# W_down and most of W_O as 512-column products in four column tiles, with six W_O rows loaded early

## The chip, the cores and the metric

The kernel runs on one core of a Trainium2 chip. The metric is the time of one execution on the device, in microseconds (us), median over runs. "Span" is the time from the first to the last instruction in the profiled execution.

## What is computed

A decoder layer with attention and a gated feed-forward network side by side, for four sequences (B = 4) with one new token each, all weights and caches in bf16:

```python
x  = A_x                                  # 4 x 1 x 512
xn = _layernorm(x)
# attention: 32 query heads, 8 key/value heads of 128, the last 4096 positions of the cache
q  = (xn @ wq) ; scores = q k^T * Dh**-0.5 ; p = softmax(scores) ; o = p v
A  = o.reshape(B, 1, 4096) @ wo           # wo: 4096 x 512
# feed-forward: 512 -> 1792 -> 512
Bf = (silu(xn @ w_gate) * (xn @ w_up)) @ w_down
return x + A + Bf                         # 4 x 1 x 512
```

The caches are 16384 positions long; only the last 4096 are read, 4 MB of K and 4 MB of V for each of the 8 key/value heads. With the weights that is 81 MB.

## The kernel before, in words

Each engine has its own program, written out in order by hand; semaphores join them. There is no scheduler: what stands first in an engine's program is done first.

**SyncE (L228 to L261)** issues nearly all loads on one queue, and the transfers run in that order: W_Q, W_gate, W_up, the two halves of the first K (L247, L248), the V of the last head group into a buffer of its own (`VL`, L250; it held W_Q before), and then for each head group g = 1 to 7 the two halves of K(g) and V(g-1) (L251 to L254), each as soon as TensorE has read what the buffer held before. There is one K buffer (two halves) and one V buffer, `VB`. Behind the last of these come W_down (L255) and W_O in five pieces, cut at the rows in `WOS` (L256, L257). W_O is laid out as 32 rows (`NR`) of 128 x 512: row e holds one of 32 slices of the contraction.

**TensorE** runs a loop of eight passes (L472), one for each head group: transposes of K (L401) and scores (L414) in turn, products that keep TensorE busy while it would wait (`spin`, L454: they multiply ones, and no result is used), then `pv` (L437) with the probabilities of the *pass before* and its V, the sums of the probabilities (L441), the shift by the maximum (L426), and `fin` (L449, L450). In `pv` the product for position t is 32 rows of output by 128 columns, in column tile t % 4 of the array, at partitions 32 (t % 4) of PSUM.

Behind the loop stands the tail: `pv` for the last group with `VL` (L491), `down` (L465), `fin`, four products that bring the attention output into the order of W_O's rows (L496), and W_O (L499 to L502). `down` and W_O go through `acc` (L459): for each row four products, one for each quarter of the 512 output columns, 4 rows of output by 128 columns. Quarter n is summed at partitions 32n to 32n + 3 of one PSUM region of 128 columns. x itself is added there too, by four fp32 products with an identity (L468); `xf` is its fp32 copy, made by VectorE (L308).

**VectorE** and **ScalarE** copy transposed K from PSUM (L322, L272), and do maxima, exponentials (L277) and normalisation (`norm`, L337 to L347). At the end VectorE writes `OP`, W_O's left operands (L363), and casts the sum to the output `y` (L365); two output transfers each on SyncE's and ScalarE's queue follow.

**GpSimd (L178 to L226)** clears buffers and makes constants; TensorE's first products wait for them (`s_const`, L217), and its first `pv` for `s_zero` (L226).

## Time and profile before

| | us |
|---|---|
| runs: median (lowest, highest) | 200.7 (200.62, 202.83) |
| profiled execution | 200.38 |
| its span, first to last instruction | 198.3 |
| TensorE busy in the span | 158.2 (80%) |
| VectorE busy | 103.4 (52%) |
| ScalarE busy | 63.0 (32%) |
| GpSimd busy | 16.7 (8%) |
| HBM read | 81.01 MB, 408 GB/s over the span |

The profile is of one execution, and 2.1 us of its time lie outside the span. In the profile's rows a line number is that of the kernel before; PE is TensorE's matmul, PEld its weight loads, DVE VectorE, ACT ScalarE, POOL GpSimd, SP SyncE. "Issue" is time in which an engine waited for nothing that the profile shows. The granted clock is the share of TensorE's full clock that the chip allowed in a stretch; q8 in the list of transfers is the queue that brings program to the engines.

### The profile page before, as it was taken

To read this page: it belongs to the slowest core of one execution; us is meant where nothing else is said; L and a number is where in the kernel's file an instruction comes from. 1 tells how busy PE (TensorE), PEld (TensorE's weight loads), DVE (VectorE), ACT (ScalarE), POOL (GpSimd) and SP (SyncE) were. 2 spreads that over 40 slices of the span, in tenths; PEclk is the share of its full clock that TensorE was granted. 3 is DMA by queue.
4 is the path that set the end of the run, shared out by engine and by line. 5 is a ranking of instruction groups with operands and counts; after the bars stand their busy time and mean duration, and the time that the engine had idled before them with its cause. 6 is when DMAs were issued, how large, how long until landed. Compare 5 with 4: busy or idle time off the path is not lost.

```text
span 198.3 us, 8645 instructions
## 1 busy us (share of the span) xinstructions
PE 158.2 (80%) x3852; PEld 136.0 (69%) x3852; DVE 103.4 (52%) x210; ACT 63.0 (32%) x85; POOL 16.7 (8%) x43
## 2 busy tenths in 40 slices
PE   0138679797998899599979986999989689978644
PEld 0138679754995697579857956698689368956544
DVE  4304047740785578147835880478468706872020
ACT  2200004503560573046415620464345115624000
POOL 8699000000000000000000000000000000000000
PEclk9999999969999999799999995799999969999975
DMA  6999999999999999999999999999999999999960
GB/s 219 430 425 437 425 426 469 433 390 433 433 418 406 430 439 439 423 449 439 420 413 446 453 420 413 436 436 420 430 466 436 397 426 473 430 394 438 409 245 1
DMA packets 4801, 81.14 MB, mean 409 GB/s; under 512 B 564, under 2 KB 568, under 8 KB 1080
## 3 DMA queue, kind: packets, MB, share of 16 engines
q1 hardware_dynamic: 4768, 81.01, 95.7%
q8 instruction: 7, 0.11, 0.2%
q14 instruction: 2, 0.02, 0.0%
q10 hardware_dynamic: 24, 0.01, 0.0%
HBM read 81.01 MB, written 0.00 MB: 408 GB/s over the span
## 4 chain that ended last, share of the span: by engine, by line
DMA 61%; PE 30%; issue 4%; DVE 2%; SPq 1%; DVEq 0%
DMA vbuf<-in_A_v_cache_dram 49%; DMA kbuf<-in_A_k_cache_dram 13%; PE ps_o L437 11%; PE ps_kt L401 8%; PE ps_s L414 3%; PE ps_s L461 3%; PE ps_kt L454 2%; PE ps_s L426 1%; PE ps_kt L441 1%; DVE kT L322 1%; PE ps_o L450 0%; PE ps_o L449 0%; DVE den L341 0%; DVE oT L346 0%; DVE oP L363 0%
## 5 line engine op out<-in xcount | busy, mean ns | idle before, releaser
L401 PE MATMUL ps_kt<-ident,kbuf 128*128 128x128 bf16 x1024 | 76.4, 221 | 2.8 <-DMA kbuf<-in_A_k_cache_dram 2.8
L322 DVE COPY kT<-ps_kt 128x1024 bf16<-128x1024 bf16 x88 | 57.6, 687 | 18.5 <-PE ps_kt L401 18.5
L401 PEld LDWEIGHTS ps_kt<-ident,kbuf 128*128 128x128 bf16 x1024 | 59.5, 98 | 5.4 <-DMA kbuf<-in_A_k_cache_dram 4.4
L272 ACT ACTIVATE kT<-ps_kt 128x1024 bf16<-128x1024 bf16 x40 | 41.0, 1025 | 38.1 <-PE ps_kt L401 38.1
L414 PE MATMUL ps_s<-qC,kT 128*128 128x16 bf16 x1024 | 44.8, 170 | 3.9 <-DVE kT L322 2.1
L414 PEld LDWEIGHTS ps_s<-qC,kT 128*128 128x128 bf16 x1024 | 36.8, 96 | 6.0 <-DVE kT L322 4.1
L437 PE MATMUL ps_o<-vbuf,p 128*32 128x128 bf16 x1024 | 20.5, 251 | 10.8 <-DMA vbuf<-in_A_v_cache_dram 9.3
L437 PEld LDWEIGHTS ps_o<-vbuf,p 128*32 128x32 bf16 x1024 | 18.9, 114 | 11.8 <-issue 11.8
L326 DVE TENSOR_REDUCE mx<-ps_s 128x16 f32<-128x512 f32 x32 | 22.1, 689 | 5.9 <-PE ps_s L414 3.6
L274 ACT ACTIVATE osb<-ps_o 128x128 f32<-128x128 f32 x8 | 2.2, 278 | 58.3 <-PE ps_kt L441 58.3
L454 PE MATMUL ps_kt<-own,ones 128*128 128x512 bf16 x64 | 17.4, 397 | 0.0
L277 ACT ACTIVATE p<-ps_s 128x512 bf16<-128x512 f32 x32 | 16.5, 602 | 0.7 <-PE ps_s L426 0.5
L339 DVE TENSOR_REDUCE dsum<-ps_kt 128x16 f32<-128x256 f32 x8 | 3.4, 425 | 25.2 <-PE ps_kt L441 25.2
L426 PE MATMUL ps_s<-cm,own 128*128 128x512 bf16 x32 | 9.5, 426 | 0.0
L454 PEld LDWEIGHTS ps_kt<-own,ones 128*128 128x128 bf16 x64 | 5.9, 109 | 4.3 <-issue 0.8
L341 DVE RECIPROCAL den<-ps_o 128x16 f32<-128x16 f32 x8 | 2.1, 258 | 12.0 <-PE ps_o L450 12.0
L380 PE MATMUL ps_s<-xnT,vlast 128*128 128x4 bf16 x128 | 3.6, 166 | 5.0 <-DMA vlast<-in_A_wq_dram 5.0
L380 PEld LDWEIGHTS ps_s<-xnT,vlast 128*128 128x128 bf16 x128 | 3.5, 104 | 5.0 <-issue 5.0
L225 POOL MEMSET vbuf<- 128x8192 f32 x1 | 6.9, 6928 | 0.0
L373 PE MATMUL ps_s<-i,xn 4*128 4x4 f32 x4 | 0.6, 261 | 7.7 <-POOLq L217 7.7
L281 ACT ACTIVATE ex<-ps_o 128x56 f32<-128x56 f32 x1 | 0.2, 218 | 19.0 <-PE ps_o L387 19.0
L426 PEld LDWEIGHTS ps_s<-cm,own 128*128 128x128 bf16 x32 | 2.7, 105 | 4.6 <-issue 3.2
(81 smaller groups left out, 84.3 us busy)
## 6 DMA issues: line engine op xcount, KB each, us to landing
kbuf<-in_A_k_cache_dram SPq DMA_DIRECT2D x16, 2048.0 KB, 14.0
vbuf<-in_A_v_cache_dram SPq DMA_DIRECT2D x7, 4096.0 KB, 15.8
vlast<-in_A_wq_dram SPq DMA_DIRECT2D x1, 4096.0 KB, 12.4
vlast<-in_A_v_cache_dram SPq DMA_DIRECT2D x1, 4096.0 KB, 25.7
wo_sb<-in_A_wo_dram SPq DMA_DIRECT2D x1, 2048.0 KB, 23.7
wg_sb<-in_B_w_gate_dram SPq DMA_DIRECT2D x1, 1792.0 KB, 16.3
wu_sb<-in_B_w_up_dram SPq DMA_DIRECT2D x1, 1792.0 KB, 21.0
wd_sb<-in_B_w_down_dram SPq DMA_DIRECT2D x1, 1792.0 KB, 19.5
```

What stands on the lines that cost most here:

```text
L225: eng.memset(VB[:].rearrange("p t d -> p (t d)").bitcast(FP32), 0.0)
L272: eng.activation(KT[:, c % 4], kt_ps[c % 3], ACT.Copy).then_inc(s_ea, 1)
L277: eng.activation(P[:, BT * q:BT * (q + 1), :], ps_S[q][:].rearrange("p (t n) -> p t n", n=NH), ACT.Exp, scale=SCALE).then_inc(s_p, 1)
L322: eng.tensor_copy(KT[:, c % 4], kt_ps[c % 3]).then_inc(s_ev, 1)
L326: eng.tensor_reduce(mx[:, q, :], ps_S[q][:].rearrange("p (t n) -> p n t", n=NH), AX.X, ALU.max)
L380: last = mm(q_ps[:, h * B:(h + 1) * B], WQ[:, c, h * Dh:(h + 1) * Dh], XnT[:, c, :], start=(c == 0 and h == 0), stop=(c == NC - 1), skip_g ...
L401: last = eng.transpose(kt_ps[c % 3][:, k, :], KB[:, CH * c + k, :], ident[:])
L414: last = mm(ps_S[q][:, NH * t:NH * (t + 1)], KT[:, c % 4, k, :], QC[:], start=(t == 0), stop=False, skip_group_check=True)
L426: mm(ps_S[q][:].rearrange("p (t n) -> p t n", n=NH), own[:], CM[:].unsqueeze(1).to_broadcast([128, BT, NH]), start=False, stop=True, skip_ ...
L437: mm(O_ps[32 * n:32 * n + 32, :], P[:, t:t + 2, :].rearrange("p t n -> p (t n)"), V[:, t, :], start=(t < 4), stop=(t >= NT - 4), skip_grou ...
L454: mm(ps_kt[2][:], ones[:], own[:].unsqueeze(1).to_broadcast([128, 4, 128]), skip_group_check=True)
L461: last = mm(acc_ps[32 * n:32 * n + B, :], left, right[:, HD * n:HD * (n + 1)], start=start, stop=stop, skip_group_check=True)
```

## The change

`down` and the first 22 rows of W_O use one product of 512 columns for each row. Row t goes to column tile t % 4, as in `pv`, so that four partial sums of the whole 4 x 512 output stand in one PSUM bank (`acc4_ps`), at partitions 32n. The left operands `guT` and `OP` are widened to 32 columns, of which 28 are zero. Behind row 21 ScalarE copies the bank to SBUF (`S2`), and four fp32 products with a selecting matrix (`sel4`) add the four partial sums into the old region `acc_ps`, behind rows 22 to 26. Rows 22 to 31 use `acc` as before.

x is not multiplied any more: ScalarE loads it in the output's layout (`X4`, four loads, behind `s_const`), and VectorE adds it as it writes `y`. `xf` and its copy go.

The first W_O piece becomes rows 0 to 5, and its load moves to just behind that of `VL`, ahead of the second K; the second piece is rows 6 to 21.

Two `spin` products are put behind the tail's `fin`, and two behind the products of L496. GpSimd clears `X4`, `sel4`, `guT` and `OP` ahead of `s_const`, and makes `sel4` behind it.

```diff
-    WOS = (0, 16, 22, 27, 30, 32)
+    WOS = (0, 6, 22, 27, 30, 32)
+    WOE = 22
...
-    OP = sb("oP", [128, NR, B], BF16)
+    OP = sb("oP", [128, NR, 32], BF16)
+    X4 = sb("x4", [128, D // 4], BF16)
+    S2 = sb("s2", [128, D], FP32)
+    sel4 = sb("sel4", [128, B], FP32)
...
-    guT = sb("guT", [128, NF, B], BF16)
+    guT = sb("guT", [128, NF, 32], BF16)
...
+    acc4_ps = ps_S[1]
...
+    x4_ap = A_x.rearrange("b s (n c) -> n (b s) c", n=4)
...  GpSimd, ahead of s_const
+            eng.memset(X4[:], 0.0)
+            eng.memset(sel4[:], 0.0)
+            eng.memset(guT[:].rearrange("p t b -> p (t b)"), 0.0)
+            eng.memset(OP[:].rearrange("p t b -> p (t b)"), 0.0)
...  GpSimd, behind it, for each n
+                select(sel4[:], [[-1, B]], ALU.not_equal, 1.0, -32 * n, 1)
...  SyncE
             eng.dma_start(VL[:], kv_ap(A_v_cache, HKV - 1, 0, NT)).then_inc(d_vl, 16)
+            load_wo(0, WOS[0], WOS[1])
             for g in range(1, HKV):
...
-            for q in range(5):
+            for q in range(1, 5):
                 load_wo(q, WOS[q], WOS[q + 1])
...  ScalarE
+            eng.wait_ge(s_const, 1)
+            for n in range(4):
+                eng.dma_start(X4[32 * n:32 * n + B, :], x4_ap[n]).then_inc(d_x4, 16)
...
+            eng.wait_ge(s_e, 1)
+            eng.activation(S2[:], acc4_ps[:], ACT.Copy).then_inc(s_ec, 1)
...  VectorE
-            eng.tensor_copy(xf[:], X[:])
...
             eng.wait_ge(s_acc, 1)
-            eng.tensor_copy(y[:], acc_ps).then_inc(s_y, 1)
+            eng.wait_ge(d_x4, 64)
+            eng.tensor_tensor(y[:], acc_ps, X4[:], ALU.add).then_inc(s_y, 1)
...  TensorE
+            def acc4(n, left, right, start, stop):
+                return mm(acc4_ps[32 * n:32 * n + 32, :], left, right, start=start, stop=stop, skip_group_check=True)
...
-                acc(I4[:], xf[:], True, False)
                 for t in range(NF):
-                    acc(guT[:, t, :], WD[:, t, :], False, False)
+                    acc4(t % 4, guT[:, t, :], WD[:, t, :], t < 4, False)
...
             fin(HKV)
+            spin(2)
             eng.wait_ge(s_nrm, HKV + 2)
...
             last.then_inc(s_pm, 1)
+            spin(2, 1)
             eng.wait_ge(s_pc, 1)
             for q in range(5):
                 eng.wait_ge(d_wo[q], 16)
                 for e in range(WOS[q], WOS[q + 1]):
-                    last = acc(OP[:, e, :], WO[:, e, :], False, e == NR - 1)
+                    if e < WOE:
+                        last = acc4(e % 4, OP[:, e, :], WO[:, e, :], False, e >= WOE - 4)
+                    else:
+                        last = acc(OP[:, e, 0:B], WO[:, e, :], e == WOE, e == NR - 1)
+                if WOS[q + 1] == WOE:
+                    last.then_inc(s_e, 1)
+                if q == 2:
+                    eng.wait_ge(s_ec, 1)
+                    acc(sel4[:], S2[:], False, False)
             last.then_inc(s_acc, 1)
```

More of the change, by code (lines that the diff above doesn't have):

```diff
@@ L67, in bass_parallel_sum__sliding_block_cached__swiglu_ffn__decode_kernel @@
     xn = sb("xn", [B, D], FP32)
-    xf = sb("xf", [B, D], FP32)
     st_sum = sb("st_sum", [B, 1], FP32)
@@ L125, in bass_parallel_sum__sliding_block_cached__swiglu_ffn__decode_kernel @@
     d_x = sem("d_x")
+    d_x4 = sem("d_x4")
     d_wq = sem("d_wq")
@@ L161, in bass_parallel_sum__sliding_block_cached__swiglu_ffn__decode_kernel @@
     s_pc = sem("s_pc")
+    s_e = sem("s_e")
+    s_ec = sem("s_ec")
     s_acc = sem("s_acc")
@@ L355, in _ @@
             eng.drain()
-            eng.tensor_tensor(guT[:], up_ps.rearrange("p (t b) -> p t b", b=B), gs[:], ALU.mult).then_inc(s_guT, 1)
+            eng.tensor_tensor(guT[:, :, 0:B], up_ps.rearrange("p (t b) -> p t b", b=B), gs[:], ALU.mult).then_inc(s_guT, 1)
             group(0)
@@ L362, in _ @@
             eng.wait_ge(s_pm, 1)
-            eng.tensor_copy(OP[:].rearrange("p r b -> p b r"), perm_ps.rearrange("p (b r) -> p b r", b=B)).then_inc(s_pc, 1)
+            eng.tensor_copy(OP[:, :, 0:B].rearrange("p r b -> p b r"), perm_ps.rearrange("p (b r) -> p b r", b=B)).then_inc(s_pc, 1)
             eng.wait_ge(s_acc, 1)
-            eng.tensor_copy(y[:], acc_ps).then_inc(s_y, 1)
+            eng.wait_ge(d_x4, 64)
+            eng.tensor_tensor(y[:], acc_ps, X4[:], ALU.add).then_inc(s_y, 1)
         @block.tensor
@@ L450, in fin, with spin @@
                 mm(O2_ps, Osb[:], sel[:, 0:NH], start=True, stop=True, skip_group_check=True).then_inc(s_fin, 1)
-            def spin(n):
+            def spin(n, k=2):
                 for _ in range(n):
-                    mm(ps_kt[2][:], ones[:], own[:].unsqueeze(1).to_broadcast([128, 4, 128]),
+                    mm(ps_kt[k][:], ones[:], own[:].unsqueeze(1).to_broadcast([128, 4, 128]),
                        skip_group_check=True)
             HD = D // 4
+            def acc4(n, left, right, start, stop):
+                return mm(acc4_ps[32 * n:32 * n + 32, :], left, right, start=start, stop=stop, skip_group_check=True)
             def acc(left, right, start, stop):
```

## The prediction

> **What bounds the kernel now.** I read the page first, then the chain that ended last, the timeline of the last 20 us, the transfers, and the clock by stretch. The page's slices say that the transfers run without a pause until the end:

> ```profile
> DMA  6999999999999999999999999999999999999960
> ...
> wo_sb<-in_A_wo_dram SPq DMA_DIRECT2D x1, 2048.0 KB, 23.7
> wo_sb<-in_A_wo_dram SPq DMA_DIRECT2D x1, 768.0 KB, 25.5
> wo_sb<-in_A_wo_dram SPq DMA_DIRECT2D x1, 640.0 KB, 26.6
> wo_sb<-in_A_wo_dram SPq DMA_DIRECT2D x1, 384.0 KB, 27.0
> wo_sb<-in_A_wo_dram SPq DMA_DIRECT2D x1, 256.0 KB, 27.2
> ```

> The slices (40 of the 198.3 us span) are nine tenths or more from the second to the third last. The last pieces (lines: tensor, KB, us from issue to landing) were issued here:

> ```profile
> 162.70 0.54 SPq L239 DMA_DIRECT2D vbuf<-in_A_v_cache_dram  x1
> 163.27 0.60 SPq L255 DMA_DIRECT2D wd_sb<-in_B_w_down_dram  x1
> 163.92 2.33 SPq L242 DMA_DIRECT2D wo_sb<-in_A_wo_dram  x5
> ```

> The first W_O piece lands at 163.92 + 23.7 = 187.6, the second at 164.4 + 25.5 = 189.9, the third at 191.5, the fourth at 192.4; the fifth, issued at about 165.8, at 193.0. The kernel ends 2.8 us after that with TensorE still working, so the end is set by TensorE's work behind the last V load. The chain shows it (start, length, what):

> ```profile
> 142.17 16.94 DMA vbuf<-in_A_v_cache_dram
> ...
> 162.70 15.83 DMA vbuf<-in_A_v_cache_dram
> ...
> 183.29 1.97 PE ps_o L437 x128
> 185.26 0.22 PE ps_kt L441 x8
> 185.48 1.10 PE ps_s L461 x56
> 186.57 3.06 issue
> 189.64 0.28 PE ps_s L461 x8
> 189.92 0.33 PE ps_o L449 x2
> 190.25 0.24 PE ps_o L450 x2
> ...
> 191.70 0.45 DVE oP L363
> ...
> 192.20 3.65 PE ps_s L461 x69
> ...
> 195.87 0.29 DVE y_sb L365
> ```

> Two things are odd there. In the middle of W_down TensorE stands still for 3.06 us with nothing to wait for; and 128 W_O products take 3.65 us (28 ns each), while 48 W_down products of the same shape took 0.84 us (17.5 ns). Stretches explain both (from:to, length, busy time and records of TensorE, the first two of W_down and W_O alone; granted clock, DMA share, GB/s; last, from the packets of 187.0 to 188.5, those that carry program):

> ```profile
> 185.73:186.57 0.84, 0.84 (x52) 1.00 0.94 397
> 192.20:195.84 3.64, 3.63 (x128) 0.50 0.02 7
> ...
> 187.50:190.90 3.40, 0.83 (x12) 1.00 0.96 389
> 190.90:194.30 3.40, 2.39 (x88) 0.50 0.20 78
> q8 instruction: 1, 0.02, 3.7%
> ```

> An instruction packet (0.02 MB) was in transit inside the stall: TensorE had run out of program. With 0.83 us of work in 187.5 to 190.9 the granted clock fell to half, and all of W_O ran at half.

> Where will it run out next? A product is two instructions (weight load and matmul), an fp32 product four. The loop's first pass has two such stalls:

> ```profile
> 39.51 0.18 PE L414 MATMUL ps_s<-qC,kT 128*128 128x16 bf16 x1 [1.20 <-issue]
> ...
> 43.41 1.78 PE L437 MATMUL ps_o<-vbuf,p 128*32 128x128 bf16 x86
> 46.60 0.79 PE L437 MATMUL ps_o<-vbuf,p 128*32 128x128 bf16 x42 [1.41 <-issue]
> ```

> **The change, part by part.** Times are in the span of this profile.

> (1) 768 KB of W_O move from behind the last V load to ahead of the second K. SP's order is the transfers' order, so the 14 later K halves, seven V loads and W_down land later; what follows the last V shrinks as much. V lands at 159.11 and 178.53: 8192 KB in 19.42 us, so 768 KB is 1.82 us; the same 768 KB cost 2.3 us at the end (187.6 to 189.9). I take 1.82: the queue is never empty (a K half needs 14.0 us from issue to landing, 4.9 of them its own), so the shift isn't absorbed. Last V: 180.35. Last W_O rows: still 193.0, as the bytes ahead of them are the same. **+1.82.**

> (2) From V's landing to the end of the last V stage: 185.48 - 178.53 = 6.95, unchanged: 187.30.

> (3) W_down: 4 fp32 products (x) and 56 of 128 columns become 14 of 512 columns, spread over four column tiles. No such product is in the trace. The nearest is L441: eight products of 256 columns on four tiles in 0.22 us, 0.11 a round of four; 512 columns make 0.22. From below 3.5 rounds, 0.77; from above 14 one after another at 0.22 (below, L454), 3.1. I take four rounds, 0.88, because L441 and L437 (128 products in 1.97, 15 ns each) already overlap four tiles with a moving operand each. Before it was 1.10 + 3.06 + 0.28 = 4.44. The stall leaves this place because a hundred instructions ahead of it go. W_down ends at 188.18. **-3.56.**

> (4) To the first W_O product: 192.20 - 189.92 = 2.28, kept: 190.46. The four added spins lie under VectorE:

> ```profile
> 126.67 0.66 PE ps_kt L454 x3
> ...
> 191.09 0.23 DVE L346 TENSOR_TENSOR oT<-on,dq 128x64 bf16<-128x64 f32 x1
> 191.70 0.44 DVE L363 CAST oP<-ps_kt 128x128 bf16<-128x128 f32 x1 [0.38 <-PE ps_kt L496]
> ```

> Two cost 0.44 at full clock, under the 0.83 from 190.49 (the end of L450) to 191.32 and then under 0.44; at half clock they stick out by about 0.4. The wider oP and guT hold the same elements: nothing.

> (5) W_O. 22 products in six rounds, 1.32: 191.78 (their rows are there by 189.9). Then ScalarE copies 128x512 fp32:

> ```profile
> L277 ACT ACTIVATE p<-ps_s 128x512 bf16<-128x512 f32 x32 | 16.5, 602 | 0.7 <-PE ps_s L426 0.5
> L461 PE MATMUL ps_s<-xf,i 4*4 4x128 f32 x8 | 0.4, 268 | 0.0
> ```

> 0.60 and two hand-overs, 0.1: 192.48. Behind the new wait stand the combining products and rows 27 to 31, and for them VectorE and the output; rows 22 to 26 (20 products, 0.35) run under the copy. Combining is four fp32 products of 128 columns: 0.40 by the x product: 192.88. Their contraction is 128 rows, not 4; should rows count, at most the 0.57 of L449 and L450. Rows 27 to 29 take 0.21; rows 30 and 31 land at 193.0 and take 0.14: 193.23. The loads (193.16) and the work (193.23) now meet; 3.64 becomes 2.77. **-0.87.**

> (6) Start. GpSimd clears 1600 more bf16 columns ahead of the constants' release:

> ```profile
> 7.72 0.64 PE L373 MATMUL ps_s<-i,xn 4*128 4x4 f32 x4 [7.72 <-POOLq L217]
> 10.66 1.82 POOL L224 MEMSET p<- 128x2064 bf16 x1
> 13.34 3.55 PE L380 MATMUL ps_s<-xnT,vlast 128*128 128x4 bf16 x128 [4.98 <-DMA vlast<-in_A_wq_dram]
> ```

> 0.88 ns a column makes 1.5 us; TensorE idles 5 us for W_Q behind it, so nothing. Past 3.5 us it would be on the path. ScalarE's four 1 KB loads of x, behind the same release, land a hundred microseconds before VectorE's add needs them. The add takes the place of the cast, 0.29; its bound is 0.2 to 0.4.

> Sum: 1.82 - 3.56 - 0.87 = -2.61. The profiled execution took 200.38 us (span 198.3), so 197.8; the median of the runs, 200.7, is 0.3 above it, so **198.1 us**. (A measurement of this kernel tells about 2%, 4 us, from no change.)

> [...]

> **Rivals.** A: *half clock in the tail*. Three of the seven V waits were followed by a stretch of 3.4 to 6.8 us at half, the dips of the page's clock row (40 slices) at 80, 120 and 160 us; the second row is one of them (columns: length, busy of TensorE, its weight loads, VectorE, ScalarE, GpSimd, clock, DMA share, GB/s):

> ```profile
> PEclk9999999969999999799999995799999969999975
> ...
> 81.70:85.10 3.40, 3.38 (x129) 3.40 (x133) 0.00 (x0) 0.00 (x0) 0.00 (x0) 0.50 1.00 429
> ...
> 177.20:180.70 3.50, 2.27 (x138) 2.02 (x137) 0.94 (x5) 0.00 (x0) 0.00 (x0) 1.00 0.92 394
> ```

> The last V wait had no such stretch behind it before (2.27 us of work in it); moved by 1.8 us it may. 3.4 us at half lose 1.7: 199.8. [...]

> B: *the program runs out inside W_O*. Counting the new tail, the boundary lies 59 instructions into W_O: 22 products and seven or eight of rows 22 and 23, reached at 191.9. The block before is entered at 184.3 + 1.82 = 186.1; with 5.4 us the next is there at 191.5, just in time; with the loop's 7.1 us at 193.2. Then the rest of rows 23 to 26 (0.22), combining (0.40) and 20 products (0.35) follow it: 194.2, 199.1 us.

> C, the other side: *512-column products of different tiles don't overlap*. W_down would take 3.1 and the 22 rows 4.8, 5.7 more in all: about 203.8, slower than before. It costs the whole gain from 0.48 us a round instead of 0.22 on, ten rounds in all. L441 and L437 speak against it.

> D: *the loads end sooner*, as the 768 KB cost 2.3 at the end and 1.82 early: landing at 192.5, while the work alone still ends at 193.2, and at 193.0 with 3.5 and 5.5 tiled rounds in place of whole ones: 197.9. The low ends of copy, combining and add (0.3 together) make 197.6. Nothing here reaches -2% (196.7) unless the transfers themselves get faster.

> **How the numbers follow.** Forecast (with D) 0.52, A 0.22, B 0.14, C 0.07, faster transfers 0.05. The low end of the unknown costs is 197.6, and 197.1 with half a microsecond for transfers that don't repeat exactly; A with the spins sticking out by 0.4 and a little more is 200.6; B lies between. Faster by over 2% is those 0.05 and as much again for what no row shows: 0.10. Slower by over 2% is most of C, at a half clock: 0.06. The rest, 0.84, is within 2%.

> **What would show it.** Right: last V landing near 180.4; no idle in W_down, which takes 0.8 to 0.9; clock 1.00 over W_O; 22 products in about 1.3; last rows' products waiting for their load near 193.0; ScalarE's copy of 0.6. Wrong: a W_down or W_O round well over 0.3 us (C); a new idle of TensorE in row 23 with an instruction packet beside it (B); 0.50 in the clock behind the last V (A); V landing where it did, which would mean that the shift was absorbed.

## The result, and the profile after

The changed kernel took 198.87 us (median of 17 runs, 197.41 to 200.21), the kernel before 200.7 (17 runs, 199.95 to 203.33): a ratio of 0.9898, 95% interval 0.9868 to 0.9928. It is a gain of 1.0%, inside the predicted range and 0.8 us above the predicted 198.1. Medians here are over all runs of a kernel; the ratios leave out runs more than 1.5% above their kernel's fastest, so the two need not agree to the last tenth.

The profiled execution took 199.11 us, 1.27 less than that of the kernel before; the sum had 2.61. These lines of its chain (start, length, what) answer to those of before:

```profile
180.11 0.25 issue
180.35 2.84 PE ps_o L457 x128
183.19 0.43 PE ps_kt L461 x8
183.62 1.50 PE ps_s L446 x4
...
186.47 1.97 PE ps_o L457 x128
188.44 0.22 PE ps_kt L461 x8
188.66 0.86 PE ps_s L480 x14
189.51 0.33 PE ps_o L469 x2
...
191.27 0.72 DVE oP L382
...
192.03 1.49 PE ps_s L480 x22
193.53 0.02 issue
193.55 0.61 ACT s L305
...
194.20 0.70 PE ps_s L484 x28
194.90 0.02 issue
194.92 0.29 DVE y_sb L385
```

The last V lands at 180.11 (before 178.53). W_down (the first L480 row) takes 0.86 us with no idle time in it (before 4.44 with the 3.06 us stall). The 22 W_O products (the second L480 row) take 1.49 us, ScalarE's copy 0.61, the combining products and the last 20 together 0.70. What is new is ahead of that: the V product that starts at 180.35 takes 2.84 in place of 1.97, and the sums and the shift behind it are slow as well. The clock by stretch says why (from:to, length, busy time of TensorE, its weight loads, VectorE, ScalarE, GpSimd, each with its number of records; granted clock, DMA share, GB/s; the last two rows are of TensorE alone):

```profile
180.70:184.10 3.40, 3.40 (x128) 2.71 (x115) 0.42 (x1) 0.28 (x1) 0.00 (x0) 0.58 1.02 437
...
188.66:189.52 0.86, 0.86 (x15) 1.00 0.95 389
192.03:193.53 1.50, 1.50 (x40) 1.00 0.00 0
```

W_down and W_O run at full clock now; a stretch at half lies over the V stage instead (0.58 on average in the first row). From V's landing to the end of the last V stage it is 8.55 us (180.11 to 188.66), 6.95 before: 1.6 us lost, and W_O ends 1.67 us later than the sum had it (194.90 for 193.23). The loads had ended long before: the last W_O piece, issued at 165.8, landed 27.0 us later, at 192.7.

```profile
wo_sb<-in_A_wo_dram SPq DMA_DIRECT2D x1, 256.0 KB, 27.0
```

### The profile page after: what moved, and what is told of

Same layout as the page of the kernel before. It is cut to its first block, busy times and chain, and to the rows that moved or that the text cites. A ratio compares the mean times of both kernels' runs of the same rounds, so it can differ in the third digit from the quotient of the medians.

```text
span 197.4 us, 8454 instructions
## 1 busy us (share of the span) xinstructions
PE 158.3 (80%) x3748; PEld 134.3 (68%) x3748; DVE 105.6 (54%) x209; ACT 63.5 (32%) x86; POOL 18.7 (9%) x51
## 2 busy tenths in 40 slices
DMA  6999999999999999999999999999999999999960
## 4 chain that ended last, share of the span: by engine, by line
DMA 63%; PE 29%; issue 3%; DVE 2%; SPq 1%; ACT 0%; DVEq 0%
DMA vbuf<-in_A_v_cache_dram 50%; DMA kbuf<-in_A_k_cache_dram 13%; PE ps_o L457 11%; PE ps_kt L421 8%; PE ps_s L434 3%; PE ps_s L446 2%; PE ps_kt L474 1%; PE ps_kt L461 1%; PE ps_s L480 1%; DVE kT L341 1%; DVE oP L382 0%; PE ps_s L484 0%; PE ps_o L470 0%; ACT s L305 0%; PE ps_o L469 0%
## 5 line engine op out<-in xcount | busy, mean ns | idle before, releaser
L295 ACT ACTIVATE p<-ps_s 128x512 bf16<-128x512 f32 x32 | 16.5, 603 | 0.9 <-PE ps_s L446 0.8
L446 PE MATMUL ps_s<-cm,own 128*128 128x512 bf16 x32 | 10.5, 461 | 0.0
L239 POOL MEMSET vbuf<- 128x8192 f32 x1 | 6.9, 6927 | 0.0
L393 PEld LDWEIGHTS ps_s<-i,xn 4*128 4x128 f32 x4 | 0.6, 206 | 9.2 <-POOLq L230 9.2
## 6 DMA issues: line engine op xcount, KB each, us to landing
kbuf<-in_A_k_cache_dram SPq DMA_DIRECT2D x16, 2048.0 KB, 14.2
wo_sb<-in_A_wo_dram SPq DMA_DIRECT2D x1, 2048.0 KB, 24.8
wg_sb<-in_B_w_gate_dram SPq DMA_DIRECT2D x1, 1792.0 KB, 16.5
```

What stands on the lines that cost most here:

```text
L239: eng.memset(VB[:].rearrange("p t d -> p (t d)").bitcast(FP32), 0.0)
L295: eng.activation(P[:, BT * q:BT * (q + 1), :], ps_S[q][:].rearrange("p (t n) -> p t n", n=NH), ACT.Exp, scale=SCALE).then_inc(s_p, 1)
L446: mm(ps_S[q][:].rearrange("p (t n) -> p t n", n=NH), own[:], CM[:].unsqueeze(1).to_broadcast([128, BT, NH]), start=False, stop=True, skip_ ...
```

## The experiments

The question was which of the four parts (early load, 512-column products, idle products, and the program's shorter length) the 1% comes from. My theory: nearly all is the program stall that left W_down, and it left because the program got shorter. The rival: the new products. In all that follows "idle products" are matmuls whose result nobody reads, and "pad" is such products put into TensorE's start, where it waits for W_Q for 5 us:

```diff
             last.then_inc(s_xT, 1)
+            for _ in range(74):
+                mm(ps_kt[2][:, 0:4], ones[:], own[:, 0:4], skip_group_check=True)
```

Each ratio is to runs of the kernel before from the same session. The medians of those were 201.2 us (early_only, before_pad74, after_late_load, after_no_spin), 201.49 (before_pad74_again, after_pad56, after_pad74, after_pad74_late_narrow) and 201.43 (the rest), against 200.7 beside the change itself; between sessions, ratios compare better than medians. Most kernels have 4 to 7 runs, so ratios that differ by less than about 1% are not apart.

| run | median us | ratio to before (95%) |
|---|---|---|
| early_only | 202.22 | 1.0076 (1.0039, 1.0112) |
| before_pad74 | 197.3 | 0.9838 (0.974, 0.9937) |
| before_pad74_again | 198.98 | 0.9868 (0.9825, 0.9912) |
| before_early_pad74 | 198.67 | 0.9864 (0.9818, 0.991) |
| after (the change) | 198.87 | 0.9898 (0.9868, 0.9928) |
| after_late_load | 198.17 | 0.9818 (0.9726, 0.991) |
| after_no_spin | 197.81 | 0.9808 (0.9734, 0.9881) |
| after_pad56 | 203.19 | 1.0115 (1.0069, 1.0162) |
| after_pad74 | 198.93 | 0.9872 (0.9822, 0.9923) |
| after_pad74_late_narrow | 198.19 | 0.985 (0.9809, 0.9891) |
| after_pad74_narrow | 197.86 | 0.9818 (0.9765, 0.987) |
| after_pad74_narrow_no_spin | 199.98 | 0.9787 (0.973, 0.9843) |
| after_pad74_narrow_3_rows | 198.05 | 0.9834 (0.9789, 0.9879) |

### The early load alone (early_only)

```diff
-    WOS = (0, 16, 22, 27, 30, 32)
+    WOS = (0, 6, 22, 27, 30, 32)
...
+            load_wo(0, WOS[0], WOS[1])
             for g in range(1, HKV):
...
-            for q in range(5):
+            for q in range(1, 5):
```

> The kernel before with one edit: W_O rows 0 to 5 are loaded ahead of the second K, the other pieces as before. Theory (the shift isn't absorbed, and the work behind the last V sets the end): last V lands at 180.3 in place of 178.5, everything behind it 1.8 us later, the stall of 3 us in W_down still there; 202.5 us. Rival (the shift is absorbed, or the loads' end counts more than the last V): V at 178.5 to 179, time within 0.5 us of 200.7.

Measured: 202.22, ratio 1.0076. The timeline of its tail (start, length, engine, line, what, idle time before and what ended it):

```profile
180.34 1.97 PE L438 MATMUL ps_o<-vbuf,p 128*32 128x128 bf16 x128
191.21 0.38 PE L462 MATMUL ps_s<-wd_sb,guT 128*4 128x128 bf16 x8 [3.07 <-issue]
```

V's products start 1.57 us later than before and the stall is there, 3.07 us: by itself this part makes the kernel slower. By the ratio it costs 1.5 us, and the interval, 0.8 to 2.3 us, holds both the 1.57 of this trace and the 1.8 forecast.

### The kernel before, with its program moved (before_pad74, before_pad74_again)

The edit is the pad above, in the kernel before, and nothing else.

> The kernel before with 74 idle products (4 columns, results unused) put into TensorE's start, where it waits for W_Q. They only move all later program by 148 instructions, so that a block of 256 begins inside the loop and the tail's next block is fetched during the loop. Theory (TensorE's stall in W_down is a wait for program): no idle in W_down; the next block begins about 37 products into W_O and may cost 0.6 us there; W_O then ends on its last load, 193.0 + 0.2; 198.0 us, nearly all that the whole change gives, with more work and none of its products. Rival (the stall has another cause, or the gain comes from the 512-column products): 200.7 us and the 3 us idle still in W_down.

> The kernel before with 74 idle products in TensorE's start once more, for a comparison on one chip with the three others. Theory: 197.3, V0 issued by 46 us (the first pass's two stalls behind it), the last load at 192.5, W_O done by 193.0 though at half clock. Rival (the first 197.3 was luck of four runs): 198.5 or more.

Measured: 197.3 and 198.98, ratios 0.9838 and 0.9868. The tail of the first one's timeline, and the end of its chain:

```profile
185.67 0.95 PE L463 MATMUL ps_s<-wd_sb,guT 128*4 128x128 bf16 x56
188.87 0.72 PE L463 MATMUL ps_s<-wo_sb,oP 128*4 128x128 bf16 x37 [0.53 <-DVE oP L363]
190.34 2.62 PE L463 MATMUL ps_s<-wo_sb,oP 128*4 128x128 bf16 x91 [0.76 <-issue]
...
164.49 28.05 DMA wo_sb<-in_A_wo_dram
192.53 0.04 issue
192.58 0.41 PE ps_s L463 x8
```

W_down's 56 products run through in 0.95 us; the stall is gone. A shorter one (0.76) stands where it was forecast, behind exactly 37 W_O products, and the chain ends on the last load, 192.53. Counted by the rows, two instructions a product and four an fp32 product, its place lies 106 instructions behind that of the old stall (8 W_down products, two fp32 products, four products ahead of W_O, 37 of W_O). In the loop's first pass the kernel before had a stall 86 products into its V stage (at 46.60); with the pad one of 3.33 us stands behind the shift (at 49.46), 108 instructions further on. With the pad's 148 that is 254 and 256. Between the two first-pass stalls without the pad (39.51 and 46.60) it is 125 products, 250 instructions. Waits are in none of these counts; a block of 256 instructions is an estimate from them and from the 511 of the prediction. So 74 useless products bring what the whole change brings, with none of its 512-column products: the stall is a wait for program, and its removal, with that of the half clock that followed it, is the gain. The repeat is 1.7 us above the first median and agrees with its rival, luck of four runs; the ratios agree with each other. In the repeat's profile the V stage ran at half clock and W_O too:

```profile
190.24 1.22 PE L463 MATMUL ps_s<-wo_sb,oP 128*4 128x128 bf16 x37 [0.53 <-DVE oP L363]
192.01 2.62 PE L463 MATMUL ps_s<-wo_sb,oP 128*4 128x128 bf16 x91 [0.55 <-issue]
```

The same 37 products took 1.22 us there and 0.72 in the first: part of the spread over its runs, 197.2 to 201.2, is the clock's. Not all of it has to be: only one of the six runs has a trace, and by the mean granted clock of each run 197.25 us went with 0.965 and 201.16 with 0.940, but 199.47 with 0.962.

### The changed kernel, with its program moved to a bad and a neutral place (after_pad56, after_pad74)

The pad with 56 and with 74 products, in the changed kernel.

> The changed kernel with 56 idle products (4 columns, results unused) in TensorE's start. They move the program by 112 instructions, so that a block of 256 ends at the tail's first W_down product, 126 products and the sums behind where the block before was entered. Theory (a block is asked for when the one before is entered, and comes 5.4 us later): TensorE idles about 3.3 us at the start of W_down, beside an instruction packet, and all of it reaches the end, since work and loads met before: 198.9 + 3 = 202 us, and half clock over W_O where the idle time fills a stretch. Rival (the place in the program doesn't matter): 198.9.

> The changed kernel with 74 such products: the tail's whole program is fetched in or ahead of the tail's first V products, no block begins in W_down or W_O. Theory (the changed kernel had no stall in the tail left; the pad gains only by that): 198.6 to 199.1, as without it, with the last V still at 180.1 and W_O ending near 193.3 or, behind a half-clock stretch, near 194.9. Rival (idle products at the start help in another way, by the clock or by an earlier first pass, which would also explain the kernel before with them): 197.5 or less.

Measured: 203.19 and 198.93. With 56, the timeline's first W_down row and, from the packets of 188 to 190 us, those with program:

```profile
190.59 1.36 PE L482 MATMUL ps_s<-wd_sb,guT 128*32 128x512 bf16 x14 [3.57 <-issue]
...
q8 instruction: 1, 0.02, 2.8%
```

and with 74 the same products:

```profile
186.84 1.03 PE L482 MATMUL ps_s<-wd_sb,guT 128*32 128x512 bf16 x14
```

With 56 the stall is back, 3.57 us (3.3 forecast), at the very first W_down product, and it takes the clock with it (W_down 1.36 us in place of 1.03). With 18 idle products more at the same place there is none: 198.93, as without a pad, so the rival of after_pad74, that idle products at the start help in another way, did not come. The new products, the copy and the combining are the same in both. The place of the program's block border decides between 1.0115 and 0.9872.

### What the new products bring (before_early_pad74)

The kernel before with the pad of 74 and the early load, against after_pad74.

> The kernel before with the 74 idle products and W_O rows 0 to 5 loaded early: against the changed kernel with 74 idle products it lacks the 512-column products, the combining, the tail's four idle products and x by VectorE. Theory (those change the time little once no stall is left): last V 180.1, W_O from 190.6, a stall of 0.6 us some 37 products in, end of W_O at 193.7 at full clock and 194.7 at half; 198.4 to 199.4 us, within 0.5 us of the kernel it is held against. Rival (the 512-column products carry the gain): 1.5 us or more above it.

Measured: 198.67, ratio 0.9864; after_pad74 has 198.93 and 0.9872. There is no difference beyond the noise of about 1 us. Its W_O, by the timeline:

```profile
191.98 2.11 PE L464 MATMUL ps_s<-wo_sb,oP 128*4 128x128 bf16 x128 [0.53 <-DVE oP L364]
```

At full clock all 128 old products take 2.11 us, from 191.98 to 194.09. The new way takes 2.87 in the changed kernel (192.03 to 194.90): 1.49 for the tiled rows, then copy, combining and 20 more products. W_down gains about 0.35 (0.95 and the x products' 0.3 to 0.4, against 0.86), W_O loses 0.76. The 0.87 us that the prediction booked for W_O was all clock: 3.64 at half against 2.11 at full. The stall that was expected 37 products in was not there: all 128 are one row. Why it is missing here is not shown.

### The early load taken out (after_late_load)

```diff
-            load_wo(0, WOS[0], WOS[1])
...
-            for q in range(1, 5):
+            for q in range(5):
```

> The changed kernel with W_O rows 0 to 5 loaded where they were, behind W_down (pieces cut at 6, 22, 27, 30, 32). Theory (work and loads end together when nothing is late, and the early load only makes the last V late): V at 178.5, work done early, the end on the last load at 193.2 even where a half-clock stretch falls behind V; 197.9 to 198.4, that is 0.5 to 1 us under the changed kernel's 198.9. Rival (the early load is what makes the change worth it): 0.5 us or more above 198.9.

Measured: 198.17, ratio 0.9818 (0.9726, 0.991): in the direction expected, not apart from the changed kernel. The profiled execution (199.44 us) is a miss that taught most: the last V landed at 180.8, later than with the early load.

```profile
49.38 14.94 DMA vbuf<-in_A_v_cache_dram
...
163.86 16.94 DMA vbuf<-in_A_v_cache_dram
...
49.50:52.50 3.00, 3.00 (x26) 1.93 (x25) 0.14 (x1) 2.23 (x5) 0.00 (x0) 0.84 0.78 268
```

The last two columns tell it: a DMA share of 0.78 and 268 GB/s here. The changed kernel in the same stretch:

```profile
46.44 17.27 DMA vbuf<-in_A_v_cache_dram
...
49.50:52.50 3.00, 3.00 (x70) 2.94 (x68) 2.23 (x4) 0.99 (x1) 0.00 (x0) 1.00 1.10 464
```

The first V load into the shared buffer waits for the first pass of the loop, and that pass has program stalls of its own (here 0.98 and 2.49 us; 42 V products at half clock, 1.36 us in place of 0.79, come on top). Where they push its issue to 49.4 us, the second K's second half is all that is left in the queue, and the transfers fall behind. The early W_O piece is a reserve for this place, of the size of its own transfer, 1.8 us by the sum. So the prediction's "the queue is never empty" holds for the profile of before and not for every execution. With the early piece the loads of the changed kernel end at 192.7 us (issue and time to landing of the last piece); of the profiles without it, before ends them at 193.0 and before_pad74 at 192.5, but after_pad74_late_narrow at 194.3 and this one at about 194.9 (estimated: 27.9 us behind an issue at 167.0, which is 3.1 behind the last V's, as in before_pad74). The load's price, 1.6 us on the last V, is so about its worth in the runs that need it. How often that is, one profile a run can't say.

### Idle products in the tail (after_no_spin)

```diff
-            spin(2)
...
-            spin(2, 1)
```

> The changed kernel without the four idle products in the tail. Theory (they keep the clock up): without them TensorE works 2.4 of 3.4 us in the stretch ahead of W_O, and the clock over W_O falls to 0.50 in some runs, 1.5 us; median 199.0 to 200.4, and no change in runs whose clock holds. Rival (the other edits already leave too little idle time): within 0.3 us of 198.9 and 1.00 over W_O.

Measured: 197.81, ratio 0.9808 (0.9734, 0.9881); six runs, four of them at 197.5 to 198.0 and two above 200. The profiled execution is one of the two:

```profile
188.50:191.90 3.40, 2.03 (x42) 1.18 (x30) 1.51 (x5) 0.28 (x1) 0.00 (x0) 1.00 0.71 281
192.00:195.40 3.40, 3.16 (x42) 1.49 (x42) 0.18 (x1) 0.38 (x1) 0.00 (x0) 0.50 0.03 6
```

2.03 us of work in one stretch, and half clock in the next, over W_O: what the idle products are there to prevent happened without them in this execution. The median, 197.81, is below both forecasts, so what the idle products are worth stays open. Nor does the busy time of a stretch alone decide the next one's clock: in the kernel before two stretches of 3.4 us had 2.01 us of TensorE's work each, a little less than the 2.03 here, and the clock behind the first was 0.50 and behind the second 1.00 (from:to, length, busy time of TensorE, granted clock, DMA share, GB/s):

```profile
37.33:40.74 3.41, 2.01 (x52) 1.00 0.89 380
40.74:44.15 3.41, 3.21 (x45) 0.50 1.01 432
44.15:47.57 3.42, 2.01 (x118) 1.00 1.00 422
47.57:50.98 3.41, 3.41 (x43) 1.00 1.07 432
```

### Looking for a better version (after_pad74_late_narrow, after_pad74_narrow, after_pad74_narrow_no_spin, after_pad74_narrow_3_rows)

"Narrow" takes the zero columns out; "late" is the edit of after_late_load, "no_spin" that of after_no_spin, "3_rows" loads only rows 0 to 2 early:

```diff
-    OP = sb("oP", [128, NR, 32], BF16)
+    OP = sb("oP", [128, NR, B], BF16)
-    guT = sb("guT", [128, NF, 32], BF16)
+    guT = sb("guT", [128, NF, B], BF16)
...
-                return mm(acc4_ps[32 * n:32 * n + 32, :], left, ...
+                return mm(acc4_ps[32 * n:32 * n + B, :], left, ...
...  3_rows
-    WOS = (0, 6, 22, 27, 30, 32)
+    WOS = (0, 3, 22, 27, 30, 32)
```

> The changed kernel with 74 idle products in TensorE's start, all of W_O loaded behind W_down, and left operands of 4 columns in place of 32 (no zero columns; partial sums at 4 of each 32 partitions, the other rows of the combining copy meet zeros). Theory: V at 178.4, no stall, the cast of oP back from 0.71 to 0.44 us, V0 issued by 46 us so that the queue doesn't run dry, the end on the last load at 192.5 + 0.2 with slack for a half-clock stretch: 196.9 us, at or a little under the kernel before with the same 74 products (197.3). Rival (the tiled products are what counts): 196 or less, well under that kernel.

> The changed kernel with 74 idle products and left operands of 4 columns. Theory: VectorE's cast of oP back from 0.71 to 0.44 us, on the path; 0.3 us under the changed kernel with 74 idle products, 198.3 to 198.7. Rival (32 columns are needed for the tiled products' speed): rounds of four longer than 0.25 us, 198.9 or more.

> The same without the tail's four idle products. Theory (they matter only where a stretch of 3.4 us happens to lie over the tail's gaps): median within 0.3 us of the one with them, with 1.00 over W_O in some runs and 0.50 in others. Rival (they keep the clock up): 0.7 us or more above it.

> The same as the narrow one with idle products, but with only rows 0 to 2 of W_O loaded early (384 KB, 0.9 us). Theory (the early load is 1.8 us of reserve against a dry queue, paid for by a last V that is 1.8 us late): last V 179.3, loads ending at 192.3 to 193.5 as half the reserve does or doesn't suffice; 197.5 to 198.3 us. Rival (the reserve counts for nothing where the first pass's stalls are moved): V at 179.3 and 0.9 us under the narrow one in every run.

Measured: 198.19, 197.86, 199.98 and 198.05. Their intervals overlap with each other, and all but one with the changed kernel's. The one is after_pad74_narrow_no_spin (0.973 to 0.9843), and its ratio is too good: it rests on three of seven runs, and the profiled one, 200.91 us with a program stall, is not among them. None of the four is shown to be better. after_pad74_narrow came out 0.4 us under its forecast, 3_rows inside it. Narrow does one thing for certain. VectorE's cast in the changed kernel:

```profile
191.27 0.71 DVE L382 CAST oP<-ps_kt 128x128 bf16<-128x128 f32 x1 [0.36 <-PE ps_kt L519]
```

and in after_pad74_narrow:

```profile
189.45 0.44 DVE L380 CAST oP<-ps_kt 128x128 bf16<-128x128 f32 x1 [0.36 <-PE ps_kt L519]
189.94 1.46 PE L480 MATMUL ps_s<-wo_sb,oP 128*4 128x512 bf16 x22
```

Writing 4 of each 32 columns costs 0.27 us more than writing 4 of 4, on the path; the tiled products are no slower with 4 columns (22 in 1.46, 1.47 with 32). The late version's transfers fell behind again, and its products wait for their rows (timeline):

```profile
191.24 1.03 PE L479 MATMUL ps_s<-wo_sb,oP 128*4 128x512 bf16 x16 [0.35 <-DMA wo_sb<-in_A_wo_dram]
194.37 0.28 PE L483 MATMUL ps_s<-wo_sb,oP 128*4 128x128 bf16 x8 [0.30 <-DMA wo_sb<-in_A_wo_dram]
```

Its last row landed at 194.3 in place of the 192.5 expected: 196.9 for it was wrong, and the missing reserve is the likely reason. The place was another, though. The V of above was issued at 44.96 here, in time; it was the third K that was issued late, at 57.84 (56.77 in before_pad74, without the reserve too). Where the transfers lost the rest is not shown. And in two of the four profiles, no_spin's and 3_rows', the pad did not do its work; each has a stall in the last V stage (2.25 and 2.24 us). 3_rows shows (timeline, and the program packets of 185 to 187 us):

```profile
188.11 0.34 PE L457 MATMUL ps_o<-vlast,p 128*32 128x128 bf16 x9 [2.24 <-issue]
...
q8 instruction: 1, 0.02, 2.7%
```

A packet with program was in transit while the tail was running, and TensorE stood still for 2.24 us, 119 products into the last V stage. In after_pad74 a packet was in transit between 130 and 132 us, in the loop, and the stage ran through. All eight profiles with 74 idle products are of the same TensorE program up to that place; in six the stage ran through (128 products in 1.97 us), in two it did not. So whether the program behind the loop is there in time varies, and the pad is no reliable cure. What decides it stays open. No-spin's median of 199.98 is of runs from 197.0 to 203.4, some of them perhaps with this stall, and says as little about the four idle products as after_no_spin's did.

The fastest runs of all kernels but before, early_only, after_pad56 and before_early_pad74 (198.29) lie at 196.85 to 197.5 us. In before_pad74 (profiled at 197.19) the last load sets the end, at 192.53. In after_pad74_narrow (197.01) no W_O row of the timeline waits for a load, and the work behind the last V ends at 192.8. Loads and work nearly meet there, so a larger gain would seem to need both to be earlier; that was not tried.

## Why the prediction was right, point by point

- **(1) +1.82 for the early load.** The last V came 1.58 us later. Shown by itself in early_only. That the queue is never empty failed, as above: it is the part's other side, and I had not seen it.
- **(2) 6.95 us from V to the end of its stage, unchanged.** 8.55 in the profile: rival A, half clock behind the V wait, priced at 1.7 and measured at 1.6. This term is the largest part of what the profiled execution lacks to the sum. Its chance, 0.22, looks too low: in six of the fourteen profiles of this case the last V stage runs in part at half clock (128 products in 2.58 to 3.39 us in place of 1.97). The runs of the change go from 197.41 to 200.21 on both sides of the forecast, as they would with rival A in some and not in others; run by run that was not shown. So a median 0.8 us off is partly luck.
- **(3) -3.56 at W_down, 3.06 of them the stall.** 0.86 for the 14 products (0.88 forecast), no idle time. The cause is shown both ways: moving the program takes the stall out of the kernel before (before_pad74) and puts it into the changed one (after_pad56). That it left with the change was the place of the block border, not the shape of the products.
- **(4) 2.28 kept.** 2.51 (189.52 to 192.03). The step that failed is "the wider oP and guT hold the same elements: nothing": the cast took 0.72, not 0.45.
- **(5) -0.87 at W_O.** 2.87 against 2.77 forecast: the 22 products took 1.49 (1.32 forecast, 0.25 us a round in place of 0.22), copy 0.61, the rest 0.70. The size was nearly right and its account was not: before_early_pad74 does the old W_O in 2.11 at full clock, so the gain is the clock's, and the new products by themselves lose.
- **(6) Nothing at the start.** TensorE's first products begin 1.5 us later, as worked out, and W_Q's still on W_Q's landing:

```profile
9.21 0.64 PE L393 MATMUL ps_s<-i,xn 4*128 4x4 f32 x4 [9.21 <-POOLq L230]
13.20 3.55 PE L400 MATMUL ps_s<-xnT,vlast 128*128 128x4 bf16 x128 [3.36 <-DMA vlast<-in_A_wq_dram]
```

- **Rivals B, C and D.** No stall in W_O (B did not come: a packet with program was in transit at 190.7, before W_O's first product at 192.03). 512-column products of four tiles overlap (C): 0.22 to 0.25 us a round. The loads ended at 192.7, 0.3 earlier (D), and that set nothing. A block border cost 3.06 (before), 3.07 (early_only), 3.57 (after_pad56) and 2.24 us (after_pad74_narrow_3_rows) of idle time in tails, 0.76 in W_O of before_pad74, and none in W_O of the changed kernel. So the cost is hidden at some borders of these tails and not at others.

## What to carry to other kernels

Idle time of an engine that waits for nothing is a place to count instructions: if the stalls stand a multiple of one number apart (here about 256 by the counts), suspect that the engine waits for its program. Here a program that began elsewhere was worth more than faster operations. Before crediting an edit with a gain, move the program without the edit; here 74 useless products gave the same 1%. And the load moved ahead in a saturated queue cost nearly its own time on all behind it, but was a reserve where that queue ran low, so look at several executions before calling a queue full.

## What the runs showed of the hardware that I had not expected

- A cast of 128 x 128 elements from PSUM takes 0.44 us when its output runs of 4 are adjacent, and 0.71 to 0.72 when they stand 32 apart.
- Products with 4 left columns in a column tile are as fast as with 32: 22 of 512 columns in 1.46 and 1.47 us.
- A packet with program came in the loop in one execution (between 130 and 132 us in after_pad74, no stall in the last V stage) and in another in the tail (between 185 and 187 us in after_pad74_narrow_3_rows, a stall of 2.24 us), with the same TensorE program up to there.
- The clock stayed at 1.00 behind one stretch of 3.4 us with 2.01 us of TensorE's work and was 0.50 behind another with as much (both in the kernel before), and 0.50 behind one with 2.03 (after_no_spin).
- The half-clock stretch falls at other places in each execution of one kernel: the same 37 products took 0.72 us in before_pad74 and 1.22 in before_pad74_again.
